# Turning batch 1's q by DMA instead of on TensorE, with w_out, k and v loaded after it

## The chip, the cores and the metric

The kernel runs on one core of one Trainium2 chip. The metric is the device time of one execution in microseconds (us), lower is better. In the text, the engines are called by the names of the profile: PE is TensorE (matmuls; PEld is its weight load, which overlaps), DVE is VectorE, ACT is ScalarE, POOL is GpSimd and SP is SyncE. POOL and SP also issue DMAs: SP's go through the hardware queue (q1 in the profile), POOL's through the software queue (q0), and only POOL's can change the type of the data on the way.

## The reference: linear attention, then a two-layer network

The inputs are q, k, v of shape (8 batches, 8 heads, 576 positions, 64), and two weight matrices, all float32.

```
theta = pi/2 * pos/576
phi(x) = concat(relu(x)*cos(theta), relu(x)*sin(theta))      # 64 -> 128 features per head
kv  = sum over s of phi(k)[s,:] (x) v[s,:]                    # 128 x 64 for each batch and head
z   = sum over s of phi(k)[s,:]
out = (phi(q) @ kv) / (phi(q) . z + 1e-6)                     # for each batch and head
x   = out of all heads side by side                           # 4608 tokens x 512
h   = x @ w_in                                                # 512 -> 2048
y   = (h * sigmoid(1.702*h)) @ w_out                          # 2048 -> 512, the result, float32
```

## The kernel before

The kernel goes through the eight batches one after the other. PE is in use nearly all the time, and while it does the network of batch b, the other engines prepare the attention of batch b+1. All instruction orders are written out by hand (`manual_schedule`): each engine carries out its instructions in the order in which the program emits them, and waits where an instruction's data or buffer is not ready. So does each issuing queue: a DMA behind one that waits is issued later. Tiles are bfloat16 on chip, sums float32 in PSUM.

For one batch the steps are these.

- The loads. `kf`, `vf` and `qf` are float32 tiles for k, v and q of one batch; there is one of each, so that the next batch's load waits until the last reader of this batch's is done. `load` (L112) brings a whole batch with nine neighbouring positions on each partition (partition p of a half of the heads holds positions 9p to 9p+8); `load_q` (L115) brings q with four neighbouring positions on each of 128 partitions (positions 0 to 511) and the last 64 positions in a DMA of their own. `load_win(g)` and `load_wout(g)` (L121, L124) bring a quarter of a weight matrix each, 1 MB of float32 that becomes 512 KB of bfloat16 on the way.
- phi. `trig` (L138) makes the cos and sin halves of one slice of positions on DVE or ACT, into `kr` for k and into `qn0` for q. `trig_q` (L147) does it for a chunk of 128 positions in the layout of `load_q`, into `qn`, which is the same memory as `qn0`. `vcopy` (L160) turns v to bfloat16 (`vt`).
- Turning q. The products with kv need phi(q) with the features on partitions (`qT`). There are two ways. On PE: `qturn_pe` (L170) transposes 128 x 128 blocks by matmul into PSUM, and `qevac` (L177) copies them to `qT` on DVE or ACT. By DMA: `qturn_dma` (L190) is a transposing DMA on SP from `qn` straight into `qT`. Batches 0 and 1 are turned on PE, batches 2 to 7 by DMA.
- kv: `kv_mm` (L205), 72 small matmuls on PE into one `at` PSUM tile, then `kv_evac` on DVE.
- Numerator and denominator: `num_mm(c)` (L219) for a chunk of 128 positions on PE; `num_div(c)` on DVE divides into `xn`.
- Turning x: `xturn_mm` on PE and `xturn_evac` on ACT (batches 0 and 1), or `xturn_dma` on SP.
- The network: `mm1(b, fc)` (four 512-column matmuls and a gelu on ACT for one of 16 blocks `fc` of the hidden width), `mm1_tail` for the last 64 positions of batches 0 and 1, and `mm2(b, t, lo, hi)` (L321): for output tile t, the hidden blocks lo to hi, 128 x 512 each, summed in PSUM; after the last block ACT copies to `ysb` and POOL writes it out (L333).

PSUM has two pools: `pmm` with four buffers (`mm` tiles; the four `mm2` sums of a batch hold all four) and `pat` with two (`at` tiles; kv and the num tiles take turns).

The stretch that matters here is the network of batch 0, in which batch 1's attention is prepared (L418 to L481). POOL issues, right behind the four quarters of w_in: k of batch 1, quarters 0 and 1 of w_out, q, v, quarters 2 and 3 of w_out (L418 to L424). PE goes on with `mm1(0, 5)` to `mm1(0, 15)`, the tails, then 64 `mm2` matmuls in the order hidden blocks 0-3, 4-7, 8-11, 12-15, between which the transposes of q, `kv_mm` and the first num and x steps of batch 1 are put:

```
    ha = at_homes()
    qturn_pe(0, ha[0])
    qturn_pe(1, ha[1])
    qevac(0)
    qevac(1, act=True)
    mm2(0, 2, 4, 8)
```

`at_homes` (L186) makes homes for two transposes out of one `at` PSUM tile, because `pmm` is taken by the four sums. `start_block(1, opened=True)` (L481) then starts the network of batch 1 with `mm1_part`, and the loop from L484 on does the other batches.

`gate` (L127) is a tiny tile into which POOL copies one element of a tile that a DMA writes. The copy waits for that DMA, and so holds back all that POOL issues after it.

Of the kernel before, what the change touches and what calls it, by code (L numbers as in the profile page):

```python
# [9 lines left out]
F32 = mybir.dt.float32  # L10
BF16 = mybir.dt.bfloat16
# [8 lines left out]
def kernel(  # L20
# [9 lines left out]
    nc = tc.nc  # L30
    B, H, S, D = q.shape
# [4 lines left out]
    NS = S // 64  # L36
    MT = 512
    NI = H // 2
# [7 lines left out]
    pmm = ctx.enter_context(tc.tile_pool(name="pmm", bufs=4, space=PSUM))  # L46
    pat = ctx.enter_context(tc.tile_pool(name="pat", bufs=2, space=PSUM))
# [4 lines left out]
    def raw(name, dt=F32):  # L52
        return one.tile([128, NI, S], dt, name=name)

    def src_of(src, b, i0=0, i1=NI):
        return src[b, 2 * i0:2 * i1].rearrange("(i hh) (p j) d -> (hh p) i (j d)", hh=2, j=NS)

    qf = one.tile([128, 2560], F32, name="qf")
    kf, vf, vb = raw("kf"), raw("vf"), raw("vb", BF16)
    qf0 = qf[:, 0:NI * S].rearrange("p (i e) -> p i e", i=NI)  # L60
    for t, src, cut in ((kf, k, 192), (qf0, q, 256)):
# [31 lines left out]
    kr = one.tile([128, NS, NI, 128], BF16, name="kr")  # L93
    vt = one.tile([128, NS, NI, VW], BF16, name="vt")
    qn = one.tile([128, 5, H, 128], BF16, name="qn")
    qn0 = qn.rearrange("p c h f -> p (c h f)")[:, 0:NS * NI * 128].rearrange(
        "p (j i f) -> p j i f", j=NS, i=NI)
    qT = one.tile([128, H, 640], BF16, name="qT")
# [13 lines left out]
    def load(t, src, b, eng=nc.gpsimd):  # L112
        eng.dma_start(out=t, in_=src_of(src, b))

    def load_q(b, eng=nc.sync):  # L115
        eng.dma_start(out=qf[:, 0:2048].rearrange("p (h e) -> p h e", h=H),
                            in_=q[b, :, 0:512, :].rearrange("h (p c) d -> p h (c d)", c=4))
        eng.dma_start(out=qf[0:64, 2048:2560].rearrange("p (h e) -> p h e", h=H),
                            in_=q[b, :, 512:S, :].rearrange("h p d -> p h d"))

    def load_win(g):  # L121
        nc.gpsimd.dma_start(out=w_in_sb[g], in_=win_r[:, :, ts(g, 512)])

    def load_wout(g):  # L124
        nc.gpsimd.dma_start(out=w_out_sb[:, ts(g, 4), :], in_=wout_r[:, g])

    gate = const.tile([1, 4], F32)  # L127
# [4 lines left out]
    load_win(1)  # L132
    nc.gpsimd.tensor_copy(gate[0:1, 1:2], vb[0:1, 3, 0:1])
    load_win(2)
    load_win(3)


    def trig(dst, src, j, act=False):  # L138
        i = src[:, :, ts(j, 64)]
        for cs, w in enumerate((cosw, sinw)):  # L140
            o = dst[:, j, :, ts(cs, 64)]
            if act:
                nc.scalar.activation(o, i, AF.Relu, scale=w[:, j:j + 1])
            else:
                nc.vector.tensor_scalar(o, i, 0.0, w[:, j:j + 1], op0=MAX, op1=MUL)  # L145

    def trig_q(c, act=False):  # L147
        n = 128 if c < 4 else 64
        if c < 4:
            i = qf[:, 0:2048].rearrange("p (h c d) -> p c h d", h=H, c=4)[:, c]  # L150
        else:
            i = qf[0:64, 2048:2560].rearrange("p (h d) -> p h d", h=H)
        for cs, w in enumerate((cosw, sinw)):
            o, sc = qn[0:n, c, :, ts(cs, 64)], w[0:n, NS + c:NS + c + 1]
            if act:
                nc.scalar.activation(o, i, AF.Relu, scale=sc)
            else:
                nc.vector.tensor_scalar(o, i, 0.0, sc, op0=MAX, op1=MUL)  # L158

    def vcopy(i0, i1, act=False):  # L160
        o = vt[:, :, i0:i1, 0:64].rearrange("p j i e -> p i j e")
        i = vf[:, i0:i1].rearrange("p i (j e) -> p i j e", e=64)
        if act:
            nc.scalar.activation(o, i, AF.Copy)
        else:
            nc.vector.tensor_copy(o, i)

    tps = {}

    def qturn_pe(c, home=None):  # L170
        tp = pmm.tile([128, 2, NI, 128], BF16, name="mm") if home is None else home
        for j in range(2 * c, min(2 * c + 2, NS)):
            for i in range(NI):
                nc.tensor.transpose(tp[:, j % 2, i], qn0[:, j, i, :], ident)  # L174
        tps[c] = tp

    def qevac(c, act=False):  # L177
        n = min(2 * c + 2, NS) - 2 * c
        o = qT[:, :, ds(c * 128, n * 64)].rearrange("f h (j p) -> f j h p", j=n)
        i = tps.pop(c)[:, 0:n].rearrange("f j i (hh p) -> f j (i hh) p", hh=2)  # L180
        if act:
            nc.scalar.activation(o, i, AF.Copy)
        else:
            nc.vector.tensor_copy(o, i)

    def at_homes():  # L186
        t = pat.tile([128, 2, 512], F32, name="at")
        return [t[:, u].bitcast(BF16).rearrange("p (j i f) -> p j i f", j=2, i=NI) for u in range(2)]

    def qturn_dma(c):  # L190
        n = 128 if c < 4 else 64
        nc.sync.dma_start_transpose(out=qT[:, :, c * 128:c * 128 + n],
                                    in_=qn[0:n, c].rearrange("p h f -> p (h f)"))
# [54 lines left out]
    def xturn_mm(c):  # L248
        ps, xn = nums[c]
        xv = xn.rearrange("p a h e -> p (a h e)")  # L250
        for kc in range(KC):
            o = ps[:, kc // 2, ds(264 + (kc % 2) * 64, 64)].bitcast(BF16)
            nc.tensor.transpose(o, xv[:, ts(kc, 128)], ident)  # L253
# [43 lines left out]
    def mm1_tail(b, half):  # L297
        if half == 0 and b % 2 == 0:
            gt[0] = gpool.tile([128, FC, 128], BF16, name="gtail", bufs=2)
        hps = pmm.tile([128, 8, 64], F32, name="mm")  # L300
        for f in range(8):
            for kc in range(KC):
                nc.tensor.matmul(hps[:, f], w_in_of(kc, half * 8 + f), x[b][:, kc, MT:S],  # L303
                                 start=(kc == 0), stop=(kc == KC - 1))
        nc.scalar.activation(gt[0][:, ts(half, 8), ts(b % 2, 64)], hps, AF.Gelu_apprx_sigmoid)

    yp = {}
    out_j = [out[b * S:b * S + S].rearrange("(p j) d -> j p d", j=NS) for b in range(2)]

    def rows(b, t):  # L310

        if t == 4:
            return [(64 * u, 64, out_j[u][NS - 1]) for u in range(2)]
        if t > 4:
            return [(64 * u, 64, out[(w + 1) * S - 64:(w + 1) * S])
                    for u, w in enumerate((TB + 2 * (t - 5), TB + 2 * (t - 5) + 1))]
        if b < 2:
            return [(64 * u, 64, out_j[b][2 * t + u]) for u in range(2)]
        return [(0, 128, out[b * S:b * S + 512].rearrange("(p c) d -> c p d", c=4)[t])]

    def mm2(b, t, lo, hi, c0=0, c1=d_model):  # L321
        if lo == 0:
            yp[t, c0] = pmm.tile([128, d_model], F32, name="mm")
        for fc in range(lo, hi):
            w = gT[fc][:, ts(t, 128)] if t < 4 else gt[0][:, fc, :] if t == 4 else gl_t[:, fc, ts(t - 5, 128)]
            nc.tensor.matmul(yp[t, c0][:, c0:c1], w, w_out_sb[:, fc, c0:c1],  # L326
                             start=(fc == 0), stop=(fc == FC - 1))
        if hi == FC:
            ysb = ypool.tile([128, d_model], F32, name="ysb")
            nc.scalar.activation(ysb[:, c0:c1], yp[t, c0][:, c0:c1], AF.Identity)  # L330
            for p0, n, dst in rows(b, t):
                eng = nc.sync if b == B - 1 else nc.gpsimd
                eng.dma_start(out=dst[:, c0:c1], in_=ysb[p0:p0 + n, c0:c1])  # L333
# [81 lines left out]
    start_block(0)  # L415


    load(kf, k, 1)  # L418
    load_wout(0)
    load_wout(1)  # L420
    load(qf0, q, 1)
    load(vf, v, 1)
    load_wout(2)
    load_wout(3)  # L424
    for j in range(NS):
        trig(kr, kf, j)
    for fc in range(5, FC):
        mm1(0, fc)
    mm1_tail(0, 0)
    mm1_tail(0, 1)  # L430
    for j in range(5):
        trig(qn0, qf0, j)
    for j in range(5, NS):
        trig(qn0, qf0, j, act=True)
    for t in range(4):
        mm2(0, t, 0, 4)
    mm2(0, 0, 4, 8)
    mm2(0, 1, 4, 8)
    ha = at_homes()
    qturn_pe(0, ha[0])  # L440
    qturn_pe(1, ha[1])
    qevac(0)
    qevac(1, act=True)
    mm2(0, 2, 4, 8)
    mm2(0, 3, 4, 8)
    hb = at_homes()
    qturn_pe(2, hb[0])
    qturn_pe(3, hb[1])
    vcopy(0, 2)
    vcopy(2, 4, act=True)  # L450
    qevac(2)
    qevac(3, act=True)
    load_q(2, nc.gpsimd)
    load(kf, k, 2, nc.gpsimd)
    load(vf, v, 2, nc.gpsimd)
    mm2(0, 0, 8, 12)
    mm2(0, 1, 8, 12)
    hc = at_homes()
    qturn_pe(4, hc[0])
    qevac(4)  # L460
    kv_open()
    kv_mm(0, 4, vt_rhs, 0, 65)
    kv_evac(0, 4)
    mm2(0, 2, 8, 12)
    mm2(0, 3, 8, 12)
    num_mm(0)
    num_div(0)
    num_mm(1)
    num_div(1)
    x_open(1)  # L470
    mm2(0, 0, 12, 16)
    mm2(0, 1, 12, 16)
    xturn_mm(0)
    xturn_evac(1, 0)
    mm2(0, 2, 12, 16)
    xturn_mm(1)
    xturn_evac(1, 1)
    num_mm(2)
# [83 lines left out]
```

## Time and profile before

| | |
|---|---|
| median of three runs | 295.74 us (295.22 to 296.53) |
| the profiled execution: its time / its span | 295.72 us / 294.0 us |
| PE busy | 284.8 us, 97% of the span |
| DVE / ACT / POOL busy | 126.1 / 131.5 / 34.7 us |
| granted PE clock | full in all 40 slices |
| `mm2`, L326, 128x512 | 506 recorded, 372 ns mean |
| `qturn_pe` of batch 1, L174, between 40.8 and 46.5 us | 36 matmuls |
| `mm1_part` of batch 1 starts on PE | 54.06 us |

All times within the execution are counted from the start of the span. The duration of one matmul in the profile (219 ns for a transpose, 379 ns for a 512-column matmul) is longer than the time between two of them, since they are pipelined: what a row of matmuls costs is read from where it starts and where the next one does. A DMA's row gives its issue on the queue; "to landing" is the time from the start of the issue until its completion is known.

### The profile page before, as it was taken

To read this page: it belongs to the slowest core of one execution; us is meant where nothing else is said; L and a number is where in the kernel's file an instruction comes from. 1 tells how busy PE (TensorE), PEld (TensorE's weight loads), DVE (VectorE), ACT (ScalarE), POOL (GpSimd) and SP (SyncE) were. 2 spreads that over 40 slices of the span, in tenths; PEclk is the share of its full clock that TensorE was granted. 3 is DMA by queue.
4 is the path that set the end of the run, shared out by engine and by line. 5 is a ranking of instruction groups with operands and counts; after the bars stand their busy time and mean duration, and the time that the engine had idled before them with its cause. 6 is when DMAs were issued, how large, how long until landed. Compare 5 with 4: busy or idle time off the path is not lost.

```text
span 294.0 us, 6250 instructions
## 1 busy us (share of the span) xinstructions
PE 284.8 (97%) x2552; PEld 161.9 (55%) x2587; DVE 126.1 (43%) x362; ACT 131.5 (45%) x230; POOL 34.7 (12%) x68
## 2 busy tenths in 40 slices
PE   8879999999999999999999999999999999999995
PEld 4775656857454555455545554555455545565444
DVE  4674514693264825581567156725763420000000
ACT  7847653685104631463136412651175117773111
POOL 6260031500123001100110011000100010000000
PEclk9999999999999999999999999999999999999999
DMA  7999979596178965797469936995595240000322
GB/s 255 238 222 283 372 192 362 169 139 184 38 139 254 296 182 136 213 311 211 111 199 338 223 90 183 328 221 131 144 371 110 74 116 36 3 0 2 88 90 71
DMA packets 67228, 52.38 MB, mean 178 GB/s; under 512 B 47392, under 2 KB 57376, under 8 KB 67200
## 3 DMA queue, kind: packets, MB, share of 16 engines
q1 hardware_dynamic: 59824, 32.52, 43.2%
q0 software_dynamic: 7376, 19.47, 23.2%
q8 instruction: 20, 0.33, 0.4%
q14 instruction: 8, 0.07, 0.1%
HBM read 36.70 MB, written 9.44 MB: 157 GB/s over the span
## 4 chain that ended last, share of the span: by engine, by line
PE 95%; ACT 1%; issue 1%; DVE 1%; ACTq 0%
PE mm L326 42%; PE mm L276 36%; PE at L210 4%; PE mm L294 4%; PE at L223 3%; PE mm L338 3%; PE mm L303 2%; ACT g L281 1%; PE at L253 1%; DVE xn L235 1%; PE at L174 1%; PE mm L174 1%; DVE inv L233 0%; DVE den L231 0%; ACT ysb L330 0%
## 5 line engine op out<-in xcount | busy, mean ns | idle before, releaser
L326 PE MATMUL mm<-w_out_sb,g 128*128 128x512 bf16 (+1 forms) x506 | 116.2, 372 | 1.3 <-issue 0.2
L276 PE MATMUL mm<-xT,w_in 128*128 128x512 bf16 (+1 forms) x598 | 112.7, 345 | 0.5
L281 ACT ACTIVATE g<-mm 128x512 bf16<-128x512 f32 x128 | 75.6, 598 | 31.9 <-PE mm L276 31.9
L276 PEld LDWEIGHTS <-w_in 128*128 128x128 bf16 x608 | 61.8, 114 | 49.0
L326 PEld LDWEIGHTS <-g 128*128 128x128 bf16 x528 | 48.7, 98 | 49.5
L330 ACT ACTIVATE ysb<-mm 128x512 f32<-128x512 f32 (+1 forms) x37 | 21.7, 586 | 111.4 <-PE mm L326 111.4
L333 POOL DMA_DIRECT2D out_dram<-ysb x38 | 20.7, 548 | 177.2 <-ACT ysb L330 177.1
L145 DVE TENSOR_SCALAR kr<-kf,cosw 128x256 bf16<-128x256 f32 x68 | 23.7, 348 | 27.3 <-DMA kf<-in_k_dram 27.3
L235 DVE TENSOR_TENSOR xn<-at,inv 128x512 bf16<-128x512 f32 x40 | 27.7, 692 | 1.6 <-DVE inv L233 0.2
L145 DVE TENSOR_SCALAR kr<-kf,sinw 128x256 bf16<-128x256 f32 x68 | 23.8, 350 | 0.0
L231 DVE TENSOR_SCALAR den<-at 128x8 f32<-128x8 f32 x40 | 6.7, 166 | 36.9 <-PE at L223 36.9
L215 DVE CAST kvs<-at 128x520 bf16<-128x520 f32 (+1 forms) x9 | 5.8, 642 | 33.1 <-PE at L210 33.0
L223 PEld LDWEIGHTS <-qT 128*128 128x128 bf16 x320 | 14.5, 97 | 7.3
L223 PE MATMUL at<-kvs,qT 128*128 128x65 bf16 x320 | 15.9, 193 | 0.0
L158 DVE TENSOR_SCALAR qn<-qf,sinw 128x512 bf16<-128x512 f32 (+1 forms) x30 | 14.3, 477 | 0.0
L158 DVE TENSOR_SCALAR qn<-qf,cosw 128x512 bf16<-128x512 f32 (+1 forms) x30 | 14.3, 477 | 0.0
L210 PEld LDWEIGHTS <-kr 64*128 64x128 bf16 x648 | 10.2, 94 | 3.5 <-issue 3.2
L294 PE MATMUL mm<-xt,w_in 128*128 128x384 bf16 x64 | 10.6, 326 | 0.0
L326 PE MATMUL mm<-w_out_sb,gl_t 128*128 128x512 bf16 x47 | 10.5, 379 | 0.1
L338 PE MATMUL mm<-warm 128*128 128x64 bf16 (+1 forms) x114 | 8.5, 237 | 1.3 <-DVE warm L76 1.3
L294 PEld LDWEIGHTS <-w_in 128*128 128x128 bf16 x64 | 7.2, 113 | 3.3
L295 ACT ACTIVATE gl_t<-mm 128x384 bf16<-128x384 f32 x16 | 7.9, 491 | 2.4 <-PE mm L294 2.4
(60 smaller groups left out, 122.7 us busy)
## 6 DMA issues: line engine op xcount, KB each, us to landing
kf<-in_k_dram SPq DMA_DIRECT2D x5, 1152.0 KB, 6.5
vf<-in_v_dram SPq DMA_DIRECT2D x5, 1152.0 KB, 9.5
qf<-in_q_dram SPq DMA_DIRECT2D x5, 1024.0 KB, 5.7
out_dram<-ysb POOLq DMA_DIRECT2D x20, 256.0 KB, 2.6
kf<-in_k_dram POOLq DMA_DIRECT2D x2, 1152.0 KB, 10.2
vf<-in_v_dram POOLq DMA_DIRECT2D x2, 1152.0 KB, 13.7
out_dram<-ysb POOLq DMA_DIRECT2D x18, 128.0 KB, 3.2
w_in<-in_moe_w_in_dram POOLq DMA_DIRECT2D x4, 512.0 KB, 9.2
```

Of the source, the lines that this page charges most:

```text
L145: nc.vector.tensor_scalar(o, i, 0.0, w[:, j:j + 1], op0=MAX, op1=MUL)
L158: nc.vector.tensor_scalar(o, i, 0.0, sc, op0=MAX, op1=MUL)
L210: nc.tensor.matmul(st["kv", i][:, hh, ds(col, n)], kr[r, j, i, :], rhs(r, i, j), start=(j == 0), stop=(j == NS - 1))
L223: nc.tensor.matmul(ps[:, h // 4, ds((h % 4) * 65, 65)], qT[:, h, ts(c, 128)], st["kvs"][:, hh, i, 0:65], start=True, stop=True)
L235: nc.vector.tensor_tensor(xn, pv[:, :, :, 0:64], inv.unsqueeze(3).to_broadcast([128, 2, 4, 64]), op=MUL)
L276: nc.tensor.matmul(hp[fc][:, t0:t1], w_in_of(kc, fc), x[b][:, kc, t0:t1], start=(kc == 0), stop=(kc == KC - 1))
L281: nc.scalar.activation(g, hp.pop(fc), AF.Gelu_apprx_sigmoid)
L294: nc.tensor.matmul(hps, w_in_of(kc, fc), xt[:, kc, :], start=(kc == 0), stop=(kc == KC - 1))
L326: nc.tensor.matmul(yp[t, c0][:, c0:c1], w, w_out_sb[:, fc, c0:c1], start=(fc == 0), stop=(fc == FC - 1))
L330: nc.scalar.activation(ysb[:, c0:c1], yp[t, c0][:, c0:c1], AF.Identity)
L333: eng.dma_start(out=dst[:, c0:c1], in_=ysb[p0:p0 + n, c0:c1])
L338: nc.tensor.matmul(w[:, 0:cols], warm[:, 0:128], warm[:, 0:cols], start=True, stop=True)
```

## The change

q of batch 1 is loaded with `load_q` instead of `load`, by POOL, right after the third quarter of w_in and ahead of the fourth. It goes through `trig_q` on DVE and `qturn_dma` on SP, five chunks, as the later batches do. POOL then copies one element of the third chunk of `qT` into `gate`, and only after that issues w_out 0, w_out 1, k, w_out 2, v and w_out 3 in this order. `qturn_pe` and `qevac` are left out for batch 1, and with them `at_homes`.

The phi of k of batch 1 moves behind the tails, and four of its nine slices go to ACT. The `mm2` matmuls of batch 0 are regrouped: 48 of them (hidden blocks 0 to 11) now come ahead of `kv_mm`, and those of blocks 12 to 15 stand one tile ahead of the num steps, two tiles behind them, one after `num_mm(2)`. The loads of q and k of batch 2 are issued ahead of the third group, v after `vcopy`.

Because q of batch 1 now has the layout of `load_q`, its tokens come out in the order of the later batches, so `rows` writes batch 1's tiles with one DMA of 128 rows each instead of two of 64.

```diff
     load_win(2)
-    load_win(3)
...
-    def qturn_pe(c, home=None):
-        tp = pmm.tile([128, 2, NI, 128], BF16, name="mm") if home is None else home
+    def qturn_pe(c):
+        tp = pmm.tile([128, 2, NI, 128], BF16, name="mm")
...
-    def at_homes():
-        t = pat.tile([128, 2, 512], F32, name="at")
-        return [t[:, u].bitcast(BF16).rearrange("p (j i f) -> p j i f", j=2, i=NI) for u in range(2)]
...
-    out_j = [out[b * S:b * S + S].rearrange("(p j) d -> j p d", j=NS) for b in range(2)]
+    out_j = out[0:S].rearrange("(p j) d -> j p d", j=NS)
...
         if t == 4:
-            return [(64 * u, 64, out_j[u][NS - 1]) for u in range(2)]
+            return [(0, 64, out_j[NS - 1]), (64, 64, out[2 * S - 64:2 * S])]
...
-        if b < 2:
-            return [(64 * u, 64, out_j[b][2 * t + u]) for u in range(2)]
+        if b == 0:
+            return [(64 * u, 64, out_j[2 * t + u]) for u in range(2)]
...
     start_block(0)
-    load(kf, k, 1)
+    load_q(1, nc.gpsimd)
+    load_win(3)
+    for c in range(5):
+        trig_q(c)
+        qturn_dma(c)
+    nc.gpsimd.tensor_copy(gate[0:1, 2:3], qT[0:1, 0, 256:257])
     load_wout(0)
     load_wout(1)
-    load(qf0, q, 1)
+    load(kf, k, 1)
+    load_wout(2)
     load(vf, v, 1)
-    load_wout(2)
     load_wout(3)
-    for j in range(NS):
-        trig(kr, kf, j)
     for fc in range(5, FC):
         mm1(0, fc)
     mm1_tail(0, 0)
     mm1_tail(0, 1)
-    for j in range(5):
-        trig(qn0, qf0, j)
-    for j in range(5, NS):
-        trig(qn0, qf0, j, act=True)
+    for j in (0, 1, 2, 3, 4):
+        trig(kr, kf, j)
+    for j in (5, 6, 7, 8):
+        trig(kr, kf, j, act=True)
+    for g in range(2):
+        for t in range(4):
+            mm2(0, t, 4 * g, 4 * g + 4)
+    load_q(2, nc.gpsimd)
+    load(kf, k, 2, nc.gpsimd)
     for t in range(4):
-        mm2(0, t, 0, 4)
-    mm2(0, 0, 4, 8)
-    mm2(0, 1, 4, 8)
-    ha = at_homes()
-    qturn_pe(0, ha[0])
-    qturn_pe(1, ha[1])
-    qevac(0)
-    qevac(1, act=True)
-    mm2(0, 2, 4, 8)
-    mm2(0, 3, 4, 8)
-    hb = at_homes()
-    qturn_pe(2, hb[0])
-    qturn_pe(3, hb[1])
+        mm2(0, t, 8, 12)
     vcopy(0, 2)
     vcopy(2, 4, act=True)
-    qevac(2)
-    qevac(3, act=True)
-    load_q(2, nc.gpsimd)
-    load(kf, k, 2, nc.gpsimd)
     load(vf, v, 2, nc.gpsimd)
-    mm2(0, 0, 8, 12)
-    mm2(0, 1, 8, 12)
-    hc = at_homes()
-    qturn_pe(4, hc[0])
-    qevac(4)
     kv_open()
     kv_mm(0, 4, vt_rhs, 0, 65)
     kv_evac(0, 4)
-    mm2(0, 2, 8, 12)
-    mm2(0, 3, 8, 12)
+    mm2(0, 0, 12, 16)
     num_mm(0)
     num_div(0)
     num_mm(1)
     num_div(1)
     x_open(1)
-    mm2(0, 0, 12, 16)
     mm2(0, 1, 12, 16)
+    mm2(0, 2, 12, 16)
     xturn_mm(0)
     xturn_evac(1, 0)
-    mm2(0, 2, 12, 16)
     xturn_mm(1)
     xturn_evac(1, 1)
     num_mm(2)
     num_div(2)
     mm2(0, 3, 12, 16)
     start_block(1, opened=True)
```

## The prediction

> **What bounds the kernel now.** I read the page first, for the busy shares and the clock.
>
> ```profile
> PE 284.8 (97%) x2552; PEld 161.9 (55%) x2587; DVE 126.1 (43%) x362; ACT 131.5 (45%) x230; POOL 34.7 (12%) x68
> PEclk9999999999999999999999999999999999999999
> PE 95%; ACT 1%; issue 1%; DVE 1%; ACTq 0%
> ```
>
> PE is the bound over the whole span, at full clock. So time goes only where PE work goes away, and comes only where PE has to wait. Next I read the chain of work that ended last, between 33 and 55 us, where the change lies. Its columns are start, length and what.
>
> ```profile
> 33.54 2.29 PE mm L303 x64
> ...
> 36.10 4.91 PE mm L326 x22
> 41.01 0.89 PE at L174 x16
> 41.90 1.73 PE mm L326 x8
> 43.63 0.89 PE at L174 x16
> ...
> 46.25 0.22 PE at L174 x4
> 46.49 1.26 PE at L210 x72
> 47.75 0.16 issue
> 47.91 1.67 PE mm L326 x7
> 49.58 0.48 PE at L223 x16
> 50.07 1.73 PE mm L326 x8
> ```
>
> The reader is to see three things: the turns of q (L174) lie on the path with 0.89 + 0.89 + 0.22 = 2.00 us; nothing waits there for a load; and an mm2 matmul costs 1.73/8 = 0.216 us. The timeline adds that the first mm2 starts at 35.66 and batch 1's network (L276) at 54.06.
>
> The third view is the timeline and the DMA issues, cut to single issues, for when loads land.
>
> ```profile
> 13.32 1.49 POOL L122 DMA_DIRECT2D w_in<-in_moe_w_in_dram  x2
> 26.25 0.35 DVE L145 TENSOR_SCALAR kr<-kf,cosw 128x256 bf16<-128x256 f32 x1 [4.15 <-DMA kf<-in_k_dram]
> 33.83 0.35 DVE L145 TENSOR_SCALAR qn<-qf,cosw 128x256 bf16<-128x256 f32 x1 [2.76 <-DMA qf<-in_q_dram]
> 39.94 0.91 POOL L116 DMA_DIRECT2D qf<-in_q_dram  x1 [18.64 <-ACT qn L143]
> 57.98 0.48 DVE L158 TENSOR_SCALAR qn<-qf,cosw 128x512 bf16<-128x512 f32 x1
> 58.95 7.86 SPq L192 DMA_TRANSPOSE qT<-qn  x5
> ```
>
> With each issue's time to landing, POOL's loads land one behind the other: w_in 2 at 20.5 (13.32 + 7.2), w_in 3 at 23.1, k at 26.2, w_out 0 at 28.5 (15.54 + 13.0), w_out 1 at 31.0, q at 33.8, v at 36.5, w_out 2 at 39.1, w_out 3 at 41.5. The queue is a line served in order, and one load takes 2.4 to 2.6 us (weights), 2.75 to 3.1 (k, q, v). The first w_out quarter lands 7.1 us before its matmul needs it.
>
> **The change part by part.** *Removed:* 36 turns on PE, 2.00 us of the path. With them go five qevac copies (0.7 us each on DVE, 1.02 on ACT), which no PE row waited for, and four issues of batch 1's output on POOL, an idle engine: nothing.
>
> *The gate.* When does the third transpose land? (a) q's main part takes w_in 3's place behind w_in 2: 20.5 + 2.9 = 23.4. I take 2.9, between 2.5 (q's 2.8 for 1152 KB, cut to 1024) and 3.5, since its pieces are shorter. DVE is through with num_div(4) at 22.1. (b) Batch 2 shows the rest in the same layout: DVE starts trig_q at 57.98, the first transpose is issued at 58.95, the third at 61.8 and lands 3.3 later, at 65.1. That is 7.1 from q's landing, so 30.5. (c) w_in 3, now behind q, lands near 26.4, so it shares the DMA engines with the first transpose for under 1 us: +0.3, between 0 and 1.5. Together 30.8. mm1 needs w_in 3 only at block 12, about 30.1, so its move costs nothing.
>
> *w_out 0, call its landing T.* Copy and wait 0.25, so it is issued at 31.05. The nearest row is batch 2's q, issued on POOL into an almost empty queue at 39.94: 6.6 us. Less 0.35 for a shorter issue (0.56 against 0.91) and 0.45 for a shorter transfer (2.45 against 2.9) that is 5.8, my value, near the 5.7 of q on SP's queue. From below 4.5 (128 KB of output land in 2.3 on SP's queue; plus 2.45, less the 0.3 that 128 KB take), from above 7.2 (vb, 4.33 to 10.5, plus 1). T = 36.85. The first mm2 is ready at 35.66: PE waits 1.2.
>
> *Behind it.* POOL issues the six loads in 3.8 us, faster than they are served. With the places above: w_out 1 at T + 2.5, k at T + 5.5, w_out 2 at T + 7.95, v at T + 10.65, w_out 3 at T + 13.05. PE: 32 matmuls from T take 6.9, so w_out 2 makes it wait another 1.0; the third group ends at T + 11.4. vcopy needs 0.8 on DVE (i 0, 1) and 1.2 on ACT (i 2, 3, which kv_mm reaches 0.63 later): kv_mm starts at T + 11.5. k's trig (10 x 0.265 on DVE, 8 x 0.40 on ACT) ends at T + 8.8, hidden. kv_mm with its gap takes 1.42, then w_out 3 is 0.15 late, four mm2 take 0.87 and cover the kvs copy (0.70): num_mm(0) starts at T + 13.95.
>
> *num_mm(0) to batch 1's network* takes 49.42 to 54.06 = 4.64 now. After, four mm2 fewer lie in it (-0.87). But the two x turns come without matmuls between: the second waits for xn 1 (ready 2.61 after num_mm(0), 0.2 late), and num_mm(2) needs the PSUM buffer that xturn_evac frees on ACT, now behind two ysb copies (0.60 each, 0.49 apart): 0.65 late. That gives it all back; 4.64 stays.
>
> So batch 1's network starts at T + 18.6 = 55.45 against 54.06: **+1.4**. Later batches are PE work as before: batch 2's loads are issued behind v's and land by about 53, 56 and 59, ahead of their readers at 57.98, 61.9 and 66.7. The profiled execution, 295.72 us (294.0 of span and 1.7 around it), stands at the median of 295.74, so the sum is 295.72 + 1.4 = **297.1**. The saving of 2.0 is real; 1.2 + 1.0 + 0.15 of waits for loads, 0.1 for vcopy, 0.85 of waits at the x turns and 0.1 of rounding take 3.4.
>
> **A rule against the rows.** At 6 to 8 us the DMA engines were 106% to 110% on the hardware queue and the software queue moved nothing, though vb had been issued at 4.33; at 97 us they shared, 64% to 39%. The Trainium skill, page "DMA: Bandwidth & Descriptors", section "Queues, rings and completion order", says that each engine goes round between the queues that have work, a packet at a time. The row at 97 agrees, the one at 6 to 8 does not. By the rule the transposes and w_in 3 halve each other while they meet, which would make (c) about 1.0 and the sum 297.8; by the early row (c) is 0 and the sum 296.8.
>
> **The rivals.** *A, w_out in time after all (faster).* If the third transpose lands by 29.5 and w_out 0 takes 4.5 to land, T is 34.2, and PE never waits for a load: kv_mm starts at 35.66 + 48 x 0.216 = 46.0 and batch 1's network at 46.0 + 1.42 + 0.87 + 4.64 = 52.95, -1.1: **294.6**, and 293.8 if the waits at the x turns are not there either. It decides from T under 35.46. For it: in batch 2 the data of all five transposes were through at 65.6, 0.5 behind the third's landing, so the gate waits mostly for data already moved, and w_out would meet little traffic. Against it: transposes are issued 1.4 us apart and moved 190 GB/s at a full DMA share, half of the loads' 400. Two pages speak for it: "Advanced Engine Details and Errata", section "X-Bar Transpose (TRN2)", of the Trainium skill has transposes as fast as other DMAs, which these rows contradict; "DMA: Bandwidth & Descriptors", section "Anatomy of one DMA", gives 2.0 us plus the bytes at 436 GB/s, by estimate 4.4 us for a w_out quarter, and with it the sum would be 295.7. No row here is that short for 1 MB.
>
> *B, a late transpose.* Batch 2's fourth took 4.8 instead of 3.3, while the DMA engines trickled at 10 GB/s near 66.5; transposes behind loads took 5.2 to 11.5. One such delay of 1.5 to 2.5 us in the first three passes through the gate to everything behind it: +2.9 to +3.9, **299.1**. PE would then wait about 3 us in one place; at 15.8 to 18 us it already idled more than half the time with the clock at 1.00.
>
> *C, w_in 3 late.* If it is over 3.7 us later than 26.4, mm1(0, 12) stops first; the gate's chain runs meanwhile, so only what exceeds the 1.2 us of wait for w_out 0 counts: late by 5.6, say, it gives 0.7 more, **297.8**. Against it: the places of the loads in this line differ by 0.4 at most.
>
> *D, the change does nothing to the path:* the transposes on PE are gone from the program, so that would need waits of just 2.0; it lies inside the main case's spread.
>
> **How the numbers follow.** Main case 0.60, its own range 296.2 to 298.2 (T between 35.9 and 37.9); A 0.13; B 0.23; C 0.04. The predicted time is the main case's, 297.1. The range goes from 295.4 (most of A left out) to 299.3 (the worst half of B left out). About what a measurement can tell from no change is 0.5%, 1.5 us: faster means under 294.3, slower over 297.2. A lies half under 294.3: 0.07 faster. The main case lies 0.30 below 297.2 and 0.30 above; with the other half of A, 0.37 same; the rest, B and C with it, 0.56 slower.
>
> **What the changed profile would show.** L174 has no rows at 41 to 47 us. DVE's first trig_q of batch 1 starts at 23.4 (a), SP's first transpose at 24.4, POOL's gate copy at 30.8, the first mm2 at 36.9 with its wait put down to w_out, a second wait of about 1 us ahead of the 33rd mm2, kv_mm at 48.4, the second x turn and num_mm(2) late by 0.2 and 0.65, batch 1's network at 55.4. The prediction is wrong if the gate copy comes more than 1 us off, if w_out 0 needs less than 5 or more than 6.8 us from its issue, if the six loads are served closer together than 2.4 us, or if the difference at 55 us grows or shrinks later on.

## The result: 298.4 us, slower by 0.75%

The changed kernel takes 298.41 us (297.46 to 299.19, five runs) against 295.72 us for the kernel before (295.22 to 296.53): a ratio of 1.0075, 95% interval 1.0051 to 1.0098. The predicted time was 297.1, the range 295.4 to 299.3, and slower by over 0.5% had a chance of 0.56. The sign and the mechanism came out as forecast; the size was 1.4 us forecast, 2.7 measured.

The waits of PE in the changed kernel (columns: who waited for what, us in total, times, longest):

```profile
PE mm L321 <- DMA w_out_sb<-in_moe_w_out_dram: 3.0, 3, 1.6
PE at L248 <- DVE xn L230: 1.4, 2, 0.8
PE at L205 <- issue: 1.4, 1, 1.4
PE mm L333 <- DVE warm L76: 1.3, 1, 1.3
PE at L218 <- ACT xT L255: 0.5, 1, 0.5
```

The first line and the last are new: three waits for w_out, 3.0 us, and one for an x turn's copy. The other three lie before 18 us, ahead of the change. The timeline of the changed kernel shows the chain that the prediction laid out, step by step:

```profile
23.41 0.49 DVE L157 TENSOR_SCALAR qn<-qf,cosw 128x512 bf16<-128x512 f32 x1 [1.04 <-DMA qf<-in_q_dram]
24.39 6.77 SPq L187 DMA_TRANSPOSE qT<-qn  x5
30.65 0.17 POOL L418 CAST gate<-qT 1x1 f32<-1x1 bf16 x1 [14.11 <-DMA qT<-qn]
31.12 1.09 POOL L125 DMA_DIRECT2D w_out_sb<-in_moe_w_out_dram  x2 [0.30 <-issue]
37.15 3.19 PE L321 MATMUL mm<-w_out_sb,g 128*128 128x512 bf16 x14 [1.05 <-DMA w_out_sb<-in_moe_w_out_dram]
43.35 0.51 ACT L142 ACTIVATE kr<-kf,cosw 128x256 bf16<-128x256 f32 x1 [6.62 <-DMA kf<-in_k_dram]
45.80 3.61 PE L321 MATMUL mm<-w_out_sb,g 128*128 128x512 bf16 x16 [1.57 <-DMA w_out_sb<-in_moe_w_out_dram]
48.56 0.76 DVE L165 CAST vt<-vf 128x1152 bf16<-128x1152 f32 x1 [2.49 <-DMA vf<-in_v_dram]
49.37 1.26 PE L205 MATMUL at<-vt,kr 64*128 64x65 bf16 x72
51.86 0.65 PE L218 MATMUL at<-kvs,qT 128*128 128x65 bf16 x16
55.41 0.40 PE L218 MATMUL at<-kvs,qT 128*128 128x65 bf16 x8 [0.48 <-ACT xT L255]
56.51 1.24 PE L271 MATMUL mm<-xT,w_in 128*128 128x128 bf16 x16
```

No row of q's transposes on PE is left between 33 and 56 us, and POOL waits 14.11 us at the gate with six loads behind it. Batch 1's network starts at 56.51 instead of 54.06, 2.45 later. That difference is carried to the end: ACT's last copy starts at 293.25 instead of 290.81. The last 0.25 us of the 2.7 lie behind it, in the last output. PE happens to reach the tails 0.27 us later than before (33.81 instead of 33.54; over all the runs below it is between 33.5 and 34.6). This adds nothing here, since PE waits for w_out 0 in any case.

### The profile page after: what moved, and what is told of

Read it like the earlier page. It is cut to its first block, busy times and chain, and to the rows that moved or that the text cites. A ratio compares the mean times of both kernels' runs of the same rounds, so it can differ in the third digit from the quotient of the medians.

```text
span 296.7 us, 6205 instructions
## 1 busy us (share of the span) xinstructions
PE 285.5 (96%) x2551; PEld 160.0 (54%) x2551; DVE 123.5 (42%) x351; ACT 129.7 (44%) x228; POOL 33.7 (11%) x66
## 4 chain that ended last, share of the span: by engine, by line
PE 88%; DMA 7%; DVE 2%; issue 1%; POOL 1%; ACT 0%; ACTq 0%; POOLq 0%
PE mm L321 38%; PE mm L271 35%; DMA w_out_sb<-in_moe_w_out_dram 6%; PE mm L289 4%; PE at L205 3%; PE at L218 3%; PE mm L333 3%; DVE xn L230 1%; DMA qT<-qn 1%; PE mm L298 1%; PE mm L173 1%; PE at L248 1%; POOL w_out_sb L125 0%; DVE inv L228 0%; POOL kf L113 0%
## 5 line engine op out<-in xcount | busy, mean ns | idle before, releaser
L321 PE MATMUL mm<-w_out_sb,g 128*128 128x512 bf16 (+1 forms) x528 | 117.4, 372 | 3.0 <-DMA w_out_sb<-in_moe_w_out_dram 3.0
L328 POOL DMA_DIRECT2D out_dram<-ysb x34 | 18.7, 551 | 176.8 <-ACT ysb L325 172.7
L144 DVE TENSOR_SCALAR kr<-kf,cosw 128x256 bf16<-128x256 f32 x64 | 22.3, 348 | 39.5 <-DMA kf<-in_k_dram 39.5
L144 DVE TENSOR_SCALAR kr<-kf,sinw 128x256 bf16<-128x256 f32 x64 | 22.5, 351 | 0.0
L210 DVE CAST kvs<-at 128x520 bf16<-128x520 f32 (+1 forms) x9 | 5.8, 642 | 33.6 <-PE at L205 33.5
L157 DVE TENSOR_SCALAR qn<-qf,cosw 128x512 bf16<-128x512 f32 (+1 forms) x35 | 16.7, 477 | 1.0 <-DMA qf<-in_q_dram 1.0
L157 DVE TENSOR_SCALAR qn<-qf,sinw 128x512 bf16<-128x512 f32 (+1 forms) x35 | 16.7, 478 | 0.0
L205 PEld LDWEIGHTS <-kr 64*128 64x128 bf16 x648 | 10.2, 94 | 4.1 <-issue 3.5
L165 DVE CAST vt<-vf 128x2304 bf16<-128x2304 f32 (+1 forms) x7 | 8.9, 1268 | 2.5 <-DMA vf<-in_v_dram 2.5
```

The source lines that it names most:

```text
L205: nc.tensor.matmul(st["kv", i][:, hh, ds(col, n)], kr[r, j, i, :], rhs(r, i, j), start=(j == 0), stop=(j == NS - 1))
```

## The experiments

**Theories.** Mine: the turns on PE were worth 2.0 us, and the hold on w_out, k and v loses more than that, all else following from when the loads come. The rivals: that the loads and the transposes get in each other's way, so that the hold is needed; and that the new order of the mm2 matmuls, not the loads, is the loss.

**The saved term alone.**

```diff
-    ha = at_homes()
-    qturn_pe(0, ha[0])
...
-    qevac(4)
```

> The kernel before with the 36 turns of batch 1's q and their copies simply left out, so that batch 1 is computed with what batch 0 left in qT. It measures the saved term alone: 2.0 us on PE, 293.8. If part of the turns were hidden behind other waits, less: 294.5 or more.

Measured: 293.63 us (median of nine), ratio 0.9923 (0.9902 to 0.9943). The interval holds 1.7 to 2.9 us around the 2.0 of the sum; batch 1's network follows the tails' first matmul by 18.43 us (34.30 to 52.73) instead of 20.52 (33.54 to 54.06), so 2.09 us in the trace. The turns were on the path in full.

**Without the gate.**

```diff
-    nc.gpsimd.tensor_copy(gate[0:1, 2:3], qT[0:1, 0, 256:257])
```

> The changed kernel without the gate copy alone: POOL issues w_out 0, w_out 1, k, w_out 2, v, w_out 3 right behind w_in 3. My theory, that the hold on the loads is the whole loss: w_out 0 lands near 29 to 31, v by 46 even if the five transposes take 5.5 us of the DMA engines out of the line; PE waits for no load, the waits at the x turns (0.85) stay, batch 1's network starts near 53 instead of 56.5, time 294.6 (-1.1 against before). Rival, that the loads and the transposes get in each other's way: with six loads in flight the transposes take 8 to 11 us each as behind k and v in batches 3 to 7, the fifth lands past 50, num_mm waits for qT and the time stays at 296.5 or above. Rival, that the new order of the mm2 matmuls is the loss: 298.4 as with the gate.

Measured: 303.2 to 308.4 us in six runs; over the three shortest (up to 306.5) the ratio is 1.031 (1.027 to 1.036). My expectation of 294.6 was wrong by more than 8 us, and the first rival was right: in the profiled run, of 308.4 us, num_mm(1) waits 10.8 us for qT. With the mm2 matmuls spread as before as well (the edit is shown under "The order of the mm2 matmuls"):

> As the run without the gate, and the mm2 matmuls stand between kv_mm, num and x turns as in the kernel before (32 + 8 ahead of kv_mm, 8 behind it, 8 between num and the first x turn, 4 between the x turns). My theory: the 0.85 of waits at the x turns go too, all of the 2.0 that the turns on PE took is kept: 293.8 (-1.9 against before). Rival (loads and transposes in each other's way): v comes too late for the earlier kv_mm, PE waits there 1 to 3 us, time 295 to 297.

Measured: 302.93, ratio 1.0236 (1.0215 to 1.0257). Neither my 293.8 nor the rival's 295 to 297 with a wait for v came true: v landed at 40.5, long before kv_mm. PE's waits in this run have no w_out, but this:

```profile
PE at L218 <- DMA qT<-qn: 6.9, 1, 6.9
```

and the reason is in the packets of its two DMA queues between 30 and 40 us (packets, MB, share of the 16 engines' time):

```profile
q0 software_dynamic: 696, 2.90, 95.4%
q1 hardware_dynamic: 695, 0.18, 9.2%
```

The counts are equal: the two queues take turns packet by packet, and a packet of the loads has about 4200 bytes (2.90 MB / 696), one of the transposes about 260. So the transposes get 70 packets a us as long as loads are waiting. Alone, in the kernel before at 61 to 65 us, they get eleven times that, 766 a us:

```profile
q1 hardware_dynamic: 3066, 0.76, 101.5%
```

That is the pace at which SP issues them (1024 packets every 1.37 us), not the most that the DMA engines move: where a backlog of transposes ran alone, in the version that beats both below, it was 3025 packets in 3 us, some 1000 a us.

That is what the Trainium skill states on the page "DMA: Bandwidth & Descriptors", section "Queues, rings and completion order": each DMA engine goes round between its queues and switches at packet boundaries. The trace agrees in the turns, 696 to 695; a packet of that page holds several descriptors, and whether the profile counts the same thing as a packet, no run here shows. The gate is thus no mere delay: without it the transposes starve, with it the loads have to wait.

The wait of 6.9 us is not the whole loss. Behind it PE ran at half its clock:

```profile
54.64:59.30 4.66, 4.66 (x21) 2.21 (x22) 1.06 (x3) 1.18 (x3) 1.10 (x2) 0.50 0.57 114
59.30:62.00 2.70, 2.70 (x32) 1.87 (x31) 1.06 (x3) 2.09 (x5) 1.99 (x4) 1.00 0.76 165
```

The columns are stretch, us, busy time of PE, PEld, DVE, ACT and POOL, PE clock, DMA share and GB/s. Half of 4.66 is 2.3 us lost. The wait of 6.9 and these 2.3, less the 2.1 that the turns took, make 7.1; batch 1's network starts 7.2 later than before (61.29 instead of 54.06).

**Where the gate stands.** If the hold costs time and its lack costs more, an earlier gate should show both.

```diff
-    nc.gpsimd.tensor_copy(gate[0:1, 2:3], qT[0:1, 0, 256:257])
+    nc.gpsimd.tensor_copy(gate[0:1, 2:3], qT[0:1, 0, 0:1])        # c0; 128:129 for c1, 512:513 for c4
```

> The changed kernel with the gate on the fifth transpose instead of the third. The fifth landed at 32.8, the third at 30.6. My theory: all that hangs on the gate comes 2.2 us later and none of it is hidden: span 298.9, time 300.6. Rival (the gate's place matters little, the loads are slowed by transposes still under way): w_out 0 needs less than 6.0 us from its issue, and the time is 299 or less.

> The gate on the second transpose. It lands near 29.2; the loads' data start near 31.5, when the transposes are nearly through (4600 packets at 766 a us from 25.7 end at 31.7). w_out 0 lands near 35.2, PE waits for loads 1.4 us less than with the gate on the third, and the clock stays at 1.00: 296.7 to 297.1, between the gates on c0 and c2. Rival (transposes under loads cost more than the earlier gate gains): 298.4 or more.

> The changed kernel with the gate on the first transpose instead of the third, so that the loads' data start about 2.8 us earlier, near 30.1, with c3 and c4 of the transposes still to move. Theory from the run without the gate, that the two queues take turns packet by packet (transposes 766 packets a us alone, 70 beside loads): some 1200 packets are left at 30.1, c3 lands near 47 and c4 near 55 at the latest, just ahead of their num steps; w_out 0 lands at 33.8, v at 45.4, kv_mm starts at 46.4, batch 1's network at 53.5 to 54, time 295.2 to 295.7, as the kernel before. Rival, that any transpose under the loads costs as without the gate: PE waits for qT at num_mm, 298.5 or more.

| gate on | w_out 0 issued | its time to landing | v landed | after w_out 0's issue | time, us | ratio to before |
|---|---|---|---|---|---|---|
| c0 | 28.19 | 7.0 | 46.95 | 18.8 | 297.23 | 1.0047 (1.0031 to 1.0063) |
| c1 | 30.01 | 6.2 | 48.10 | 18.1 | 297.83 | 1.0057 (1.0038 to 1.0077) |
| c2 (the change) | 31.12 | 6.0 | 48.56 | 17.4 | 298.41 | 1.0075 (1.0051 to 1.0098) |
| c4 | 33.75 | 5.2 | 49.78 | 16.0 | 299.79 (one run) | |

The gate moves by 5.6 us from c4 to c0, v's landing by only 2.8. The earlier the loads start, the more transposes are still under way, and the slower is w_out 0: 5.2 us with none left, 7.0 with the most. Half of what an earlier gate gains is given back. None of the three times came out as expected. For c4, 300.6 was expected if nothing that hangs on the gate were hidden, and it came out at 299.79: w_out 0 needed less than 6.0 us, as the rival said, but the time was not 299 or less. For c1, 296.7 to 297.1 was expected and 297.83 measured, since w_out 0 landed at 36.2 and not at 35.2. For c0, 295.2 to 295.7 was expected: the transposes indeed fitted in (no wait for qT; chunk 3 landed at 49.5, chunk 4 at 56.3, somewhat later than the 47 and 55 expected), but the loads were slowed too, which I had not counted. The differences between neighbouring gates are within their intervals; the table rests on the landings.

The gate on c4 shows the fall of the clock once more, behind a shorter wait (columns as above):

```profile
36.00:39.00 3.00, 0.00 (x1) 0.01 (x1) 0.00 (x0) 0.46 (x1) 3.00 (x5) 1.00 1.08 203
39.50:43.00 3.50, 3.50 (x10) 1.25 (x9) 0.00 (x0) 0.00 (x0) 0.00 (x0) 0.52 1.02 333
43.50:46.00 2.50, 2.50 (x13) 1.16 (x12) 1.50 (x6) 1.50 (x4) 0.00 (x0) 1.00 1.08 235
```

After a wait of 3.17 us PE runs at about half its clock for some 3.5 us. Most of that is hidden: the second wait for w_out is gone in this run, eaten by slower matmuls. But not all of it. With the gates on c0, c1 and c2, kv_mm starts 0.81 us after v has landed; here v lands at 49.78 and kv_mm waits for the 48 mm2 matmuls in front of it:

```profile
39.00 12.22 PE L321 MATMUL mm<-w_out_sb,g 128*128 128x512 bf16 x48 [3.17 <-DMA w_out_sb<-in_moe_w_out_dram]
51.15 1.26 PE L205 MATMUL at<-vt,kr 64*128 64x65 bf16 x72
```

That is 1.37 us after v, so by estimate 0.56 of the time with this gate is the clock's and not the gate's. In the changed kernel, where the waits are 1.05 and 1.57, these stretches show a clock of 1.00.

**Which load sets the pace.**

```diff
     load_wout(1)
-    load(kf, k, 1)
     load_wout(2)
+    load(kf, k, 1)
     load(vf, v, 1)
```

> The changed kernel with w_out 2 loaded ahead of k instead of behind it; v keeps its place. My theory, that v's landing sets when kv_mm starts: the wait of 1.57 us for w_out 2 goes, but PE then waits about as much longer for vcopy ahead of kv_mm, which starts at 49.3 as before; time 298.4, no change (within 0.3). Rival, that each wait for w_out is lost by itself: 1.2 to 1.6 us faster, 297. It also shows once more how long w_out 1 takes behind w_out 0 after the gate: 3.3 us if that belongs to loads into an empty queue, 2.5 if it was chance.

Measured: 297.77, ratio 1.0068 (1.0044 to 1.0093), where the change had 1.0075: no change that can be told apart, as expected. PE's waits show the shift from w_out 2 to v's copy:

```profile
PE mm L321 <- DMA w_out_sb<-in_moe_w_out_dram: 1.5, 1, 1.5
PE at L205 <- DVE vt L165: 0.8, 1, 0.8
```

Its two waits come to 2.3 where the change has 3.0 for w_out and none for vt. In this run w_out 1 came sooner behind w_out 0 (2.4 us instead of 3.3), which is taken up below. The same order with the gate on c0:

> Gate on the first transpose and w_out 2 ahead of k. If the waits for loads are all that is lost and transposes fit in beside the loads: w_out 0 at 33.8 and w_out 2 at 39 are early enough for PE never to wait for a weight, v lands at 44.5, kv_mm starts at 45.6, batch 1's network at 52.7, time 294.2 (-1.5 against before). If the transposes left over are starved: num_mm(3) or num_mm(4) waits and the time is 296 or above.

Measured: 297.49, ratio 1.0064 (1.0039 to 1.0089), not 294.2. PE has no wait for w_out 0 to 2 here, and still waits 1.5 us for vt, since v lands at 47 and not at 44.5. With the loads slowed by the transposes, neither of the two orders that were tried behind the gate beats the kernel before.

**The order of the mm2 matmuls.**

```diff
-    for t in range(4):
-        mm2(0, t, 8, 12)
+    mm2(0, 0, 8, 12)
+    mm2(0, 1, 8, 12)
...
     kv_evac(0, 4)
-    mm2(0, 0, 12, 16)
+    mm2(0, 2, 8, 12)
+    mm2(0, 3, 8, 12)
     num_mm(0)
...
     x_open(1)
+    mm2(0, 0, 12, 16)
     mm2(0, 1, 12, 16)
-    mm2(0, 2, 12, 16)
     xturn_mm(0)
     xturn_evac(1, 0)
+    mm2(0, 2, 12, 16)
     xturn_mm(1)
```

> The changed kernel, gate and loads as they are, with the mm2 matmuls spread between kv_mm, num and x turns as in the kernel before. The waits at the x turns (0.85) go, but kv_mm, which waits for v at 49.3 in any case, then has 24 mm2 behind it instead of 16: 49.3 + 7.57 = 56.9 for batch 1's network against 56.5 now: 298.8, no gain. Rival, that the bunched x turns are a loss by themselves: 297.5.

Measured: 298.58, ratio 1.0092 (1.0073 to 1.0111), as expected and no gain. PE waits 1.7 us for vt instead of 0.5 for the x turn's copy. The bunched x turns are not a loss by themselves, as long as v comes so late.

**A version that beats both.** If 2.0 us are to be had, and transposes move at full speed only without loads beside them, they belong where no urgent load is in the line. In the kernel before that is just behind w_out 3: the next loads are batch 2's, which nobody reads before 57 us. So this version keeps the loads' old order, takes q in `load_q`'s layout at its old place, turns it by DMA, and holds back batch 2's loads instead of w_out, k and v:

```diff
-    load(qf0, q, 1)
+    load_q(1, nc.gpsimd)
     load(vf, v, 1)
     load_wout(2)
     load_wout(3)
     for j in range(NS):
         trig(kr, kf, j)
+    for c in range(5):
+        trig_q(c)
+        qturn_dma(c)
...
+    nc.gpsimd.tensor_copy(gate[0:1, 2:3], qT[0:1, 0, 512:513])
     load_q(2, nc.gpsimd)
     load(kf, k, 2, nc.gpsimd)
     load(vf, v, 2, nc.gpsimd)
```

The PE transposes and their copies are left out, the mm2 matmuls stay where they were, and `rows` is as in the change.

> The kernel before with its loads in their old order; q of batch 1 comes in the layout of load_q at its old place in the line, is turned by DMA, and the loads of batch 2 (not w_out, k and v of batch 1) are held until the fifth transpose has landed. My theory (hardware and software queue take turns packet by packet, 70 transposing packets a us beside loads and 766 alone; the turns on PE are worth 2.0): the first transpose is issued near 35; 350 of its 1024 packets move until the loads end near 41.5, the rest alone: chunk 0 lands near 43, chunk 2 near 46, the fifth near 48, each ahead of its num step (47.5, 47.7, 51, 53, 54); batch 2's loads land by 60, ahead of their readers; no new wait on PE: 293.8 (-2.0). Rival, that turning by DMA beside the network's loads always costs more than it saves: 296 or above, with a wait for qT at num_mm.

Measured: 293.90 us, ratio 0.9935 (0.9919 to 0.9952). Its timeline:

```profile
35.24 27.26 SPq L192 DMA_TRANSPOSE qT<-qn  x7
44.40 1.26 PE L210 MATMUL at<-vt,kr 64*128 64x65 bf16 x72
47.32 0.65 PE L223 MATMUL at<-kvs,qT 128*128 128x65 bf16 x16
48.47 0.17 POOL L440 CAST gate<-qT 1x1 f32<-1x1 bf16 x1 [24.47 <-DMA qT<-qn]
49.04 0.91 POOL L116 DMA_DIRECT2D qf<-in_q_dram  x1 [0.40 <-DVE den L231]
51.97 1.24 PE L276 MATMUL mm<-xT,w_in 128*128 128x128 bf16 x16
```

The first five transposes are issued from 35.24 on; the row runs on to batch 2's. Between 36 and 41 us they move 309 packets beside 275 of the loads, and then 3025 between 42 and 45. The chunks landed at 43.4, 44.3, 45.3, 47.8 and 48.4, where 43 to 48 was expected. num_mm starts at 47.32 without a wait, and batch 1's network at 51.97, 2.09 us ahead of the kernel before. The counter-proof is the same without the hold:

> The same without the hold on batch 2's loads: q, k and v of batch 2 are issued behind w_out 3 and stand beside the transposes until about 53. My theory: 70 packets a us until then, so chunk 0 lands near 51 and chunk 1 near 55, num_mm(0) waits some 3.5 us and num_mm(1) some 4 more: 300 or above. Rival, that the starving came from w_out's large pieces alone and batch 2's q, k and v leave room: within 1 us of the run with the hold.

Measured: 310.86 in the one run, with this wait at num_mm(1):

```profile
PE at L223 <- DMA qT<-qn: 13.4, 1, 13.4
```

It was longer than I had worked out (some 7.5 us in two places), in one place, and the PE clock was at 0.50 between 60 and 67.5 us, when PE had work again.

## Why the prediction was right, and where its size was off

| step of the prediction | forecast | measured |
|---|---|---|
| turns on PE, saved | 2.00 | 2.09 (trace of the run without them) |
| (a) q landed, trig_q starts | 23.4 | 23.41 |
| (b) first transpose issued | 24.4 | 24.39 |
| (c) gate copy | 30.8 | 30.65 |
| w_out 0 issued | 31.05 | 31.12 |
| T, first mm2 | 36.85 | 37.15 |
| k, after T | 5.5 | 6.20 |
| w_out 2, after T; the wait for it | 7.95; 1.0 | 8.65; 1.57 |
| v, after T | 10.65 | 11.41 |
| w_out 3, after T | 13.05 | 13.85 |
| num_mm(0), after T | 13.95 | 14.71 |
| num_mm(0) to batch 1's network | 4.64 | 4.65 |
| batch 1's network | 55.45 | 56.51 |

Every step is there, in its place. The 1.06 us that are missing at 55.45 sit in two terms. T came 0.30 late: 0.07 at the issue and 0.2 in w_out 0's time to landing (6.0 for 5.8). The other 0.76 is one term of "Behind it", the one that was mis-sized: w_out 1 landed 3.3 us after w_out 0 (issued at 31.66, 8.8 us to landing) instead of 2.5; from there on the loads kept the forecast distances (2.85, 2.45, 2.76, 2.4 against 3.0, 2.45, 2.7, 2.4). The sum puts nothing on traffic that w_out meets. What stood behind that was a reading of batch 2: all five transposes through at 65.6, 0.5 behind the third's landing. That reading was wrong. In batch 2 a part of the transposes' packets came only later, after a pause (kernel before, 60 to 66 us, then 66 to 68):

```profile
q1 hardware_dynamic: 4033, 1.01, 125.2%
q1 hardware_dynamic: 735, 0.17, 42.2%
```

The last of them moved at 67.8, 2.7 us behind the third's landing. In the changed kernel the last moved at 32.3, 1.8 behind it, when w_out was already issued. Between 31.4 and 33 us it moved:

```profile
q0 software_dynamic: 14, 0.06, 68.7%
q1 hardware_dynamic: 624, 0.14, 49.1%
```

624 transposing packets and 14 of w_out. The runs with the gate in front of w_out tell whether that tail is the cause, since they differ in how much of it is left when w_out 0 is issued. The forecast from this issue to the landing of w_out 1 was 5.8 + 2.5 = 8.3 us.

| gated run | transposing packets moved in between | w_out 0 issued to w_out 1 landed, us |
|---|---|---|
| c4 | 0 | 7.9 |
| w_out 2 first (gate on c2; w_out 0 issued 0.6 later) | 349 | 8.2 |
| c2 (the change) | 645 | 9.35 |
| c2, mm2 spread | 662 | 9.4 |
| c1 | 1449 | 9.8 |
| c0, w_out 2 first | 1639 | 10.2 |
| c0 | 1656 | 10.3 |

The time grows with the packets over all seven runs, and c4, which differs from the change in the gate's place alone, has none and takes 1.5 us less. So the tail is what held up w_out 1. How it does so is open: the change's 645 packets took 9.1% of the DMA engines' time in these 9.35 us, which is 0.85 and not 1.5.

The stretch with the x turns, where the sum set waits of 0.85 against four matmuls less, came out within 0.01 us. That "nothing else" would change later on held too: the 2.45 at 56.5 is 2.44 at the last copy.

The rivals. A (w_out in time after all) did not happen. Its lower price, 293.8 with no waits at the x turns, is right for the case that the loads come in time: without the turns the kernel is at 293.6, and 293.9 where they are done by DMA without harm. But its condition, T under 35.46, doesn't bring this about: with the gate on c0, T was 35.2, PE had no wait for w_out 0 at all, and the kernel was still slower by 0.47%, because v didn't come earlier by as much. The distances behind T, which I took as fixed in A as in the main case, stretch when the loads overlap with transposes. B (a late transpose) did not happen: the third took 3.4 us. C did not happen: w_in 3 landed at 26.3, where 26.4 was forecast.

The rule that was set against the rows, turns by packets: I gave it a price of 0.7 us for w_in 3 meeting the first transposes, and took 0.3. In the changed kernel w_in 3 had nearly gone when they started, and the third landed 7.1 us after trig_q's start as in batch 2, so (c) came out at nothing. The price was also worked out wrongly. Turns by packets do not halve two queues that meet: with packets of 4200 and 260 bytes they gave 95.4% and 9.2% of the time. And the turns, as far as these runs show them, decide everything if the gate is left out: 696 to 695 there, and 1023 to 1008 with the gate on c0 between 30 and 47 us. The early row that spoke against them (the software queue idle at 6 to 8 us) had misled me into thinking it open; why it was idle there, no run tells.

## What to carry to other kernels

A DMA's price depends on the size of its packets and on what else is in line: before moving work from a compute engine to a DMA with small packets, look in the packet counts at who shares the DMA engines in that stretch, and put it where the loads beside it are not urgent, holding back those that are not needed rather than those that are. A hold on a queue moves everything behind it; work out the last load of the chain (here v), not the first wait, since curing an earlier wait only lengthens the later one. And check a saving on the path by leaving the work out once: here it said in one run that 2.0 us were there to be had.

## What the hardware showed that I had not expected

Transposing packets of some 260 bytes and load packets of some 4200 take turns one to one, 696 to 695 in 10 us, so that a transpose, which lands after about 3.3 us alone (batch 2 before), took 20.0 and 28.6 us (the first two without the gate, mm2 spread).

PE's clock fell to about half (0.52 over 39.5 to 43 us) behind a wait of 3.17 us, and stayed at 1.00 behind waits of 1.46, 1.57 and 1.87. The Trainium skill, page "TensorE: Matmul & The Clock Gate", part 1, puts the idle window at about 3.4 us and the lower clock at a half. The trace agrees in the half; as to the window, 3.17 us, a little less, was enough. A hold that makes PE wait near 3 us can thus cost more than the wait. With the gate on c0 and w_out 2 first, the three runs with a mean clock of 0.992 to 0.994 took 298.7 to 299.1 us and the three at 1.000 took 297.0 to 297.2 (a seventh, at 0.998, 297.5); without traces of those runs it stays open whether this is the same effect.
